# Even tokens first: loading queries and keys two tokens to a partition in a block-sparse attention and mixer kernel

## The chip, the cores and the metric

The kernel runs on one core of one Trainium2 chip. The metric is the device time of one execution in microseconds (us), as the median of several runs.

## The reference, cut to what matters

The inputs are `q`, `k` and `v` of 4 batches, 8 heads, 768 tokens and 64 numbers a head, and four mixer weights, all in float32. Attention is sparse by blocks of 64 tokens. Each query scores the mean key of each of the 12 blocks, keeps the best three that are not in its future, and always keeps its own block. Inside the kept blocks it attends causally.

```
k_rep = k.reshape(B, H, n_blocks, block, D).mean(axis=3)
gate_scores = np.einsum('bhsd,bhnd->bhsn', q, k_rep)        # future blocks: -1e9
top_idx = np.argsort(gate_scores, axis=-1)[..., -top_k:]    # and the own block
scores = scale * np.matmul(q, k.transpose(0, 1, 3, 2))      # masked by block and causally
x = softmax(scores) @ v                                     # then x: (batch, 768, 512)
u = x + (relu(x.transpose(0, 2, 1) @ w_tok1) @ w_tok2).transpose(0, 2, 1)
out = u + relu(u @ w_ch1) @ w_ch2
```

The order of the 768 tokens inside the chip's memories is free as long as queries, keys, values, masks, the token weights and the stores agree on it.

## The kernel before, in words

The work is cut into 16 pairs of heads (two heads of one batch, four pairs to a batch). A pair is first prepared and then attended.

Preparation (`prepare`, called for each pair): `load_qk` (L312) loads keys and then queries of both heads in float32 on SP's queue, 128 tokens to a tile and one token to a partition, so that each contiguous piece in memory is one token of one head, 256 bytes; it issues one transfer for each head. `transposes` (L358) turns six tiles on TensorE, `evac_t` (L367) copies them out on ScalarE, and `cast` (L376, GpSimd) or `cast_act` (L383, ScalarE, pair 0 alone) writes the two heads in half precision into the slots `KA` and `QA`. `ksum` (L388) sums keys by block on VectorE and `kcopy` (L396) places the sums of the two heads. The gate follows: `gate_q` (L406, pair 0), `gate` with `gate_s` and `gate_r` (L415 to L435, single pairs), or `gate_t`, `gate_e` and `gate_b` (L437 to L463) for a group of two or four pairs (`GROUPED`, L49). On VectorE `gm` (L465) adds the bias for future blocks, `top` (L482) takes the eight largest of 12 gate scores, ten times a pair, `below` (L492) compares with the third, and `bias` (L503) makes mask numbers. `mask` (L513) transposes them on TensorE, and `put_mask` (L522) writes them as 24 extra rows below the queries; `indicator` (L337) has put matching rows below the keys, so that one matmul gives scores with the block mask in them. The first 128 queries need no mask, so there are five gate tiles (`GJ`).

Attention (`attend`): for each head, `scores` (L529) in three groups of key tiles, `expo` (L547) on ScalarE, `diag` (L555) for the causal corner of the diagonal tiles on VectorE (for pair 0 TensorE adds the corner `tri`), `av` (L563) with the values and a column of ones, `recip` and `norm` (L575, L583). `load_v` (L322) loads the values on GpSimd's queue and casts them on the way.

The mixer runs by batch: `tok1`, `relu1`, `umix`, `uadd` over tokens (in columns for batch 0), a transpose of `u` (on TensorE for batch 0, by DMA with `turn_u` after that), and `ch1`, `relu2`, `ch2`, `oadd`, `store` over channels. Token weights come in two transfers on GpSimd's queue, the first and second that L732 and L733 issue.

The order of all instructions is written out when the program is built: `plan` (L113) is a list scheduler with a cost and a priority for each operation, its own model of the transfers (`transfers`, L84) and of the buffer rings. Each engine then runs its instructions in that order. The mixer of batch 0 fills TensorE under later pairs. `AHEAD` (L27) says how far the first four pairs are prepared ahead of their attention; `VAFTER` (L44) says after which cast the load of each pair's values may be issued, and `WAIT` (L50) does it for the weights. In the first microseconds `dummy` (L721) matmuls on a constant tile fill TensorE's holes.

```
T[t32, i] = t
for g in range(2):
    nc.sync.dma_start(out=t[:, :, D * g:D * g + D], in_=src[b, h + g].rearrange("(j p) d -> p j d", p=128))
```

Of the kernel before, what the change touches and what calls it, by code (L numbers as in the profile page):

```python
# [26 lines left out]
AHEAD = 2.5  # L27
LATER = 1.0
R = 5
# [10 lines left out]
def QACT(i):  # L40
# [3 lines left out]
VAFTER = [("kt", 1), ("kt", 2), ("qt", 2), ("qt", 3), ("qt", 3), ("qt", 4), ("qt", 6), ("qt", 8),  # L44
          ("qt", 11), ("qt", 12), ("qt", 13), ("qt", 14), ("kt", 15), ("qt", 15), ("qt", 15), ("qt", 15)]
DIRECT = (0,)
WSIZE = (2400, 4500)
GATE = {1: 400, 2: 1000, 3: 1000, 4: 1000}
# [174 lines left out]
def kernel(  # L223
# [23 lines left out]
    GJ = NJ - 1  # L247
# [25 lines left out]
    ks2 = [sp.tile([128, 32], FP, tag=f"ks{r}", name=f"ks{r}") for r in range(R)]  # L273
    bn16 = [sp.tile([128, GJ, 128], F16, tag=f"bn{y}", name=f"bn{y}") for y in range(NBN)]
    w1_16 = sp.tile([128, NJ, DT], F16, tag="w1", name="w1")
    w2_16 = sp.tile([128, 2, S], F16, tag="w2", name="w2")
    wc1_16 = sp.tile([128, NCC, DC], F16, tag="wc1", name="wc1")
    wc2_16 = sp.tile([128, NFC, DM], F16, tag="wc2", name="wc2")
    own4 = sp.tile([128, 4 * GJ, 2 * NB], FP, tag="own4", name="own4")
    gbias = sp.tile([128, GJ, 2 * NB], FP, tag="gbias", name="gbias")  # L280
    gown = sp.tile([128, 3 * GJ * NB], FP, tag="gown", name="gown")
    gone = gown[:, 0:GJ * NB].rearrange("p (j n) -> p j n", n=NB)
    own = gown[:, GJ * NB:].rearrange("p (j c) -> p j c", c=2 * NB)
# [5 lines left out]
    gt = sp.tile([128, S - 128], FP, tag="gt", name="gt")  # L289
# [22 lines left out]
    def load_qk(i, t32, src):  # L312
        b, h = pairs[i]

        def f():
            t = sb(t32, [128, NJ, 2 * D], FP, f"{t32}_{i}")
            T[t32, i] = t
            for g in range(2):
                nc.sync.dma_start(out=t[:, :, D * g:D * g + D], in_=src[b, h + g].rearrange("(j p) d -> p j d", p=128))
        return f  # L320

    def load_v(i):  # L322
        b, h = pairs[i]

        def f():
            nc.gpsimd.dma_start(out=V16[i % (R + 1)].rearrange("p g j d -> p (g j) d")[:, :, 0:D],  # L326
                                in_=v[b, h:h + 2].rearrange("g (j p) d -> p (g j) d", p=128))
        return f
# [5 lines left out]
    def twice(t):  # L334
        return t.rearrange("p j (x n) -> p j x n", x=1).broadcast_to([128, GJ, 2, NB])

    def indicator(r):  # L337
        if r:
# [3 lines left out]
        nc.vector.tensor_scalar(out=KAX[64:MK, r].rearrange("q x s -> q (x s)").bitcast(FP).rearrange("q (m w) -> q m w", w=32),  # L342
                                in0=ident32[64:MK, 64:MK].rearrange("q (m w) -> q m w", w=1).broadcast_to([2 * NB, 2 * NB, 32]),
                                scalar1=ONES, scalar2=None, op0=ALU.mult)

    def own_four():
        for c in range(4):
            nc.gpsimd.tensor_copy(out=own4[:, c:4 * GJ:4, :], in_=own)
        nc.gpsimd.tensor_copy(out=gbias.rearrange("p j (x n) -> p j x n", n=NB), in_=twice(gone))
# [8 lines left out]
    def transposes(t32, i):  # L358
        def f():
            p = ps("big", None, f"t{t32}")  # L360
            T["tr", t32, i] = p
            t = T[t32, i]
            for j in range(NJ):
                nc.tensor.transpose(out=p[:, 128 * j:128 * j + 128], in_=t[:, j, :], identity=ident32)  # L364
        return f
# [10 lines left out]
    def cast(dst, name, i, x):  # L376
        def f():
            lo = 64 * x
            to, src = dst[i % R][x][0:64, :], T[name, i][lo:lo + 64, :]
            nc.gpsimd.tensor_copy(out=to, in_=src)  # L380
        return f

    def cast_act(dst, name, i, x):  # L383
        def f():
# [635 lines left out]
```

## Time and profile before

| what | us |
|---|---|
| median of three runs (263.88 to 265.19) | 264.51 |
| the profiled execution | 264.1 |
| its span, first to last instruction | 262.4 |
| TensorE matmul busy | 253.8 |
| VectorE busy | 158.1 |
| ScalarE busy | 146.4 |
| GpSimd busy | 79.8 |

The span is the part of the execution that the profile divides up; 1.7 us of the profiled execution lie around it. Engines overlap, so busy times don't add up to the span. Names: PE is TensorE's matmul, PEld its weight load, DVE VectorE, ACT ScalarE, POOL GpSimd, SP the engine that issues the loads of queries and keys and the stores; a "q" after an engine marks its issuing of transfers. Matmuls are pipelined, so that a busy PE still may have room. L364 is line 364 of the kernel. A row of the timeline gives the start, the length, the engine, the line, the operation, the tiles written and read with their sizes, and the count of instructions that were merged.

### The profile page before, as it was taken

The page shows a single profiled execution, that of the slowest core. Times are in us where ns is not written, and L with a number is a line of the kernel's source. Part 1 is how long each engine was busy: PE and PEld are TensorE (multiplying, and loading weights), DVE is VectorE, ACT ScalarE, POOL GpSimd, SP SyncE. Part 2 cuts the span into 40 slices and gives each one's busy share as a digit, 9 for nine tenths or more (in the row PEclk, how much of TensorE's full clock was granted, in tenths as well). Part 3 has the DMA queues.
Part 4 walks back from the last instruction along what each step waited for, and adds up shares of the span by engine and source line. Part 5 has one row for each costly group of instructions (what it writes and reads, how often), then busy time and mean ns, then how long its engine had stood idle before and what let it go on. Part 6 is the DMA issues. An engine that isn't in the chain of part 4 may idle for free.

```text
span 262.4 us, 5901 instructions
## 1 busy us (share of the span) xinstructions
PE 253.8 (97%) x2330; PEld 162.8 (62%) x2330; DVE 158.1 (60%) x539; ACT 146.4 (56%) x200; POOL 79.8 (30%) x112
## 2 busy tenths in 40 slices
PE   7999899999999999899999999999999999999994
PEld 7977588885776685566655766544455544466443
DVE  4569869998966499886598566462243253333222
ACT  3886998877899669677617999410034400044000
POOL 8299628974557462640730000000000000000000
PEclk9999999999999999999999999999999999999999
DMA  8999999999999974493193000008220035300032
GB/s 166 224 171 204 203 185 192 184 197 190 204 183 170 209 151 30 32 142 91 10 169 106 2 2 0 2 0 200 80 82 0 0 65 138 130 30 2 0 146 95
DMA packets 91323, 28.78 MB, mean 110 GB/s; under 512 B 84896, under 2 KB 87840, under 8 KB 91296
## 3 DMA queue, kind: packets, MB, share of 16 engines
q1 hardware_dynamic: 63232, 21.33, 38.5%
q0 software_dynamic: 28064, 7.08, 27.6%
q8 instruction: 18, 0.29, 0.5%
q14 instruction: 9, 0.07, 0.1%
HBM read 26.83 MB, written 6.29 MB: 126 GB/s over the span
## 4 chain that ended last, share of the span: by engine, by line
PE 74%; DVE 15%; DMA 5%; ACT 2%; issue 2%; POOL 1%; DVEq 0%; ACTq 0%
PE c L704 21%; PE c L683 20%; PE sps L539 10%; PE avp L571 6%; DMA V<-in_v_dram 5%; DVE QA L525 3%; DVE m L489 3%; PE avp L721 3%; PE ups L614 3%; PE tql L364 2%; PE tok L602 2%; PE tkl L364 2%; ACT e L552 1%; PE gtp L443 1%; DVE e L559 1%
## 5 line engine op out<-in xcount | busy, mean ns | idle before, releaser
L552 ACT ACTIVATE e<-sps 128x1024 f16<-128x1024 f32 (+1 forms) x96 | 84.0, 919 | 19.0 <-PE sps L539 18.1
L683 PE MATMUL c<-uT,wc 128*128 128x256 f16 (+1 forms) x384 | 69.9, 326 | 0.9 <-DVE QA L525 0.7
L704 PE MATMUL c<-wc,h 128*128 128x512 f16 (+2 forms) x300 | 64.8, 370 | 0.0
L693 ACT ACTIVATE h<-c 128x512 f16<-128x512 f32 x48 | 28.7, 598 | 58.0 <-PE c L683 57.7
L683 PEld LDWEIGHTS <-wc 128*128 128x128 f16 x384 | 36.5, 97 | 24.6 <-issue 1.1
L539 PE MATMUL sps<-QA,KA 88*128 88x512 f16 (+3 forms) x256 | 50.8, 306 | 0.9 <-ACT e L552 0.8
L704 PEld LDWEIGHTS <-h 128*128 128x128 f16 x300 | 28.8, 98 | 31.3 <-issue 0.6
L380 POOL CAST KA<-kt 64x768 f16<-64x768 f32 x30 | 25.1, 837 | 41.4 <-ACT kt L373 30.8
L712 DVE TENSOR_TENSOR ob<-u,c 128x512 f32<-128x512 f16 (+2 forms) x25 | 16.6, 666 | 34.8 <-PE c L704 34.7
L695 DVE TENSOR_SCALAR h<-c 128x256 f16<-128x256 f32 x48 | 20.3, 424 | 27.8 <-PE c L683 27.7
L559 DVE TENSOR_TENSOR e<-e,m 128x256 f16<-128x256 f16 x90 | 29.2, 333 | 13.1 <-ACT e L552 12.5
L539 PEld LDWEIGHTS <-KA 88*128 88x128 f16 x256 | 22.6, 98 | 17.1 <-issue 1.5
L380 POOL CAST QA<-qt 64x768 f16<-64x768 f32 x30 | 25.3, 842 | 11.5 <-ACT qt L373 10.1
L571 PE MATMUL avp<-V,e 128*128 128x65 f16 x672 | 26.7, 193 | 1.3 <-DVE e L559 0.9
L571 PEld LDWEIGHTS <-e 128*128 128x128 f16 x672 | 25.4, 97 | 3.8 <-DVE e L559 1.1
L373 ACT COPY kt<-tkl 128x768 f32<-128x768 f32 x16 | 12.8, 798 | 10.5 <-PE tkl L364 6.8
L393 DVE TENSOR_REDUCE kst<-kt 128x12 f32<-128x768 f32 x16 | 15.0, 945 | 6.0 <-ACT kt L373 5.9
L590 DVE TENSOR_TENSOR x<-avp,rc 128x384 f16<-128x384 f32 x32 | 17.8, 555 | 0.6
L326 POOL DMA_DIRECT2D V<-in_v_dram x16 | 16.4, 1030 | 0.0
L525 DVE COPY QA<-bps 24x640 f16<-24x640 f16 x32 | 14.2, 480 | 1.1 <-PE bps L519 0.8
L373 ACT COPY qt<-tql 128x768 f32<-128x768 f32 x16 | 12.8, 801 | 2.6 <-PE tql L364 2.4
L622 DVE TENSOR_TENSOR u<-x,ups 128x512 f16<-128x512 f16 x18 | 11.6, 683 | 3.9 <-PE ups L614 3.8
(75 smaller groups left out, 212.9 us busy)
## 6 DMA issues: line engine op xcount, KB each, us to landing
kl<-in_k_dram SPq DMA_DIRECT2D x32, 192.0 KB, 5.3
ql<-in_q_dram SPq DMA_DIRECT2D x32, 192.0 KB, 5.4
out_dram<-ob SPq DMA_DIRECT2D x23, 256.0 KB, 2.0
V<-in_v_dram POOLq DMA_DIRECT2D x16, 192.0 KB, 6.3
wc<-in_moe_w_ch_dram POOLq DMA_DIRECT2D x8, 384.0 KB, 8.4
w<-in_moe_w_tok_dram POOLq DMA_DIRECT2D x2, 384.0 KB, 8.4
out_dram<-ob SPq DMA_DIRECT2D x1, 160.0 KB, 1.8
out_dram<-ob SPq DMA_DIRECT2D x1, 96.0 KB, 1.7
```

Of the source, the lines that this page charges most:

```text
L373: nc.scalar.copy(out=t, in_=p[:, 0:S])
L380: nc.gpsimd.tensor_copy(out=to, in_=src)
L525: nc.vector.tensor_copy(out=QA[i % R][x][64:MK, 128:S], in_=T["bps", gi][32 * s:32 * s + 2 * NB, :])
L539: nc.tensor.matmul(out=p[:, off + a:off + a + n], lhsT=KA[i % R][x][0:MK, 128 * kk:128 * kk + 128], rhs=QA[i % R][x][0:MK, q0 + a:q0 + a + ...
L552: nc.scalar.activation(out=e[:, 0:width], in_=T["sps", i, x, g][:, 0:width], func=AF.Exp, scale=scale)
L559: nc.vector.tensor_tensor(out=d, in0=d, in1=m0.rearrange("p (a b) -> p a b", a=1).broadcast_to([128, 2, 128]), op=ALU.mult)
L571: nc.tensor.matmul(out=p[:, jq, :], lhsT=T["e", i, x, g][:, o:o + 128], rhs=V16[i % (R + 1)][:, x, kk, :], start=(kk == 0), stop=(kk == jq))
L590: nc.vector.tensor_tensor(out=T["x16", b][:, :, 64 * hh:64 * hh + 64], in0=T["aps", i, x][:, :, 0:64], in1=T["rc", i, x].broadcast_to([128 ...
L683: nc.tensor.matmul(out=p, lhsT=wc1_16[:, cc, 128 * fc:128 * fc + 128], rhs=T["uT", b][:, cc, a // 128:e // 128, :], start=(cc == 0), stop= ...
L693: nc.scalar.activation(out=T["h2", b][:, fc, a:e], in_=T["c1", b, fc, n], func=AF.Relu)
L695: nc.vector.tensor_scalar(out=T["h2", b][:, fc, a:e], in0=T["c1", b, fc, n], scalar1=0.0, scalar2=None, op0=ALU.max)
L704: nc.tensor.matmul(out=T["c2", b, j, lo], lhsT=T["h2", b][:, fc, 128 * j:128 * j + 128], rhs=wc2_16[:, fc, lo:hi], start=(fc == 0), stop=( ...
```

## The change

A 128-token tile now holds the even tokens of its 128 in its first 64 places and the odd ones in the last 64. Queries and keys of a pair come in one transfer for each tensor. A partition receives two neighbouring tokens of one head as one piece of 512 bytes, and a row of a loaded tile has even-token numbers in columns 0 to 63 and odd-token numbers in columns 64 to 127. A transposed tile therefore has even tokens on partitions 0 to 63 and odd ones on 64 to 127, for one head, where it had the two heads before. A cast now takes one parity of both heads, and writes 64-column runs.

All that meets tokens follows: values, the rows of `w_tok1` and the stores are cut in two by parity, one transfer each; `w_tok2` is loaded as it is and reordered on GpSimd (`turn_w2`). Key sums are made per 32 pairs of tokens, exchanged between partition halves and added (two more small reduces in `kcopy`). A gate tile now holds 128 token pairs of one head, with 12 columns for the even and 12 for the odd token, so there are six instead of five (`NM`), with twelve runs of `top` for ten; `gm` and `bias` work pair by pair inside a group, and the copies `own4` and `gbias` (`own_four` on GpSimd) are gone. `tri` and `m0` are each made in two halves. In the planner, costs follow, `AHEAD` goes from 2.5 to 3.0, five entries of `VAFTER` name earlier casts, and casts wait for the scores of both heads of the old pair.

The diff, cut to its core:

```diff
-AHEAD = 2.5
+AHEAD = 3.0
-VAFTER = [("kt", 1), ("kt", 2), ("qt", 2), ("qt", 3), ("qt", 3), ("qt", 4), ("qt", 6), ("qt", 8),
-          ("qt", 11), ("qt", 12), ("qt", 13), ("qt", 14), ("kt", 15), ("qt", 15), ("qt", 15), ("qt", 15)]
+VAFTER = [("kt", 1), ("kt", 2), ("qt", 2), ("qt", 3), ("qt", 3), ("kt", 4), ("qt", 5), ("qt", 6),
+          ("qt", 10), ("qt", 11), ("qt", 13), ("qt", 14), ("kt", 15), ("qt", 15), ("qt", 15), ("qt", 15)]
...
-            t = sb(t32, [128, NJ, 2 * D], FP, f"{t32}_{i}")
+            t = sb(t32, [128, NM, 2 * D], FP, f"{t32}_{i}")
             T[t32, i] = t
-            for g in range(2):
-                nc.sync.dma_start(out=t[:, :, D * g:D * g + D], in_=src[b, h + g].rearrange("(j p) d -> p j d", p=128))
+            nc.sync.dma_start(out=t, in_=src[b, h:h + 2].rearrange("g (c p t) d -> p (g c) (t d)", p=128, t=2))
...
-            nc.gpsimd.dma_start(out=V16[i % (R + 1)].rearrange("p g j d -> p (g j) d")[:, :, 0:D],
-                                in_=v[b, h:h + 2].rearrange("g (j p) d -> p (g j) d", p=128))
+            for t in range(2):
+                nc.gpsimd.dma_start(out=V16[i % (R + 1)][64 * t:64 * t + 64].rearrange("p g j d -> p (g j) d")[:, :, 0:D],
+                                    in_=v[b, h:h + 2].rearrange("g (j p t) d -> t p (g j) d", p=64, t=2)[t])
...
-            to, src = dst[i % R][x][0:64, :], T[name, i][lo:lo + 64, :]
-            nc.gpsimd.tensor_copy(out=to, in_=src)
+    def half(dst, i, t):
+        return dst[0:64, i % R].rearrange("p x (j t w) -> p (x j) t w", t=2, w=64)[:, :, t, :]
+    def cast(dst, name, i, t):
+        return lambda: nc.gpsimd.tensor_copy(out=half(dst, i, t), in_=pairs_of(name, i, t))
...
+            for lo in (0, 64):
+                nc.vector.tensor_reduce(out=kst[lo:lo + 64, :, 1], in_=kst[64 - lo:128 - lo, :, 0:1], axis=AX.X, op=ALU.add)
             for lo, c in ((0, 0), (64, NB)):
...
+            for s, i in enumerate(GROUPED[gi]):
+                nc.vector.tensor_tensor(out=a[:, s].rearrange("p (t m n) -> p t m n", t=2, n=NB),
+                                        in0=T["gps", i].rearrange("p m (t n) -> p t m n", n=NB),
+                                        in1=gown[:, 0].rearrange("p (t m n) -> p t m n", t=2, n=NB), op=ALU.add)
...
-            for j in range(GJ):
-                for x in range(2):
-                    nc.vector.max(out=t[:, j, s, x, :], in_=T["gm", gi][:, j, s, NB * x:NB * x + NB])
+            for r in range(2 * NM):
+                nc.vector.max(out=T["m8", gi][:, s, r, :], in_=T["gm", gi][:, s, NB * r:NB * r + NB])
...
-            for j in range(GJ):
-                nc.tensor.transpose(out=p[0:n, 128 * j:128 * j + 128], in_=bn16[gi % NBN][:, j, 0:n], identity=ident16)
+            for m in range(NM):
+                t, c = m // (NM // 2), m % (NM // 2)
+                nc.tensor.transpose(out=p[0:n, 256 * c:256 * c + 256].rearrange("q (h t w) -> q t h w", h=2, t=2)[:, t], in_=bn16[gi % NBN][:, m, 0:n], identity=ident16)
...
-        return lambda: nc.sync.dma_start(out=out[b, 128 * j:128 * j + 128, lo:hi], in_=T["ob", b, j, lo][:, 0:hi - lo])
+            for t in range(2):
+                nc.sync.dma_start(out=out[b, 128 * j:128 * j + 128, lo:hi].rearrange("(p t) c -> t p c", t=2)[t],
+                                  in_=T["ob", b, j, lo][64 * t:64 * t + 64, 0:hi - lo])
...
+    def load_w1():
+        for t in range(2):
+            nc.gpsimd.dma_start(out=w1_16[64 * t:64 * t + 64], in_=w1[t])
+    def turn_w2():
+        nc.gpsimd.tensor_copy(out=w2_16.rearrange("p g (j t w) -> p (g j) t w", t=2, w=64),
+                              in_=w2_in.rearrange("p g (j w t) -> p (g j) t w", t=2, w=64))
...
-                O["cast", name, i, x] = op("POOL", occ, occ + 55, [O[name, i]] + last_scores(x), pre + 4 + off,
+                O["cast", name, i, x] = op("POOL", occ, occ + 55, [O[name, i]] + last_scores, pre + 4 + off,
...
-    own_op = op("POOL", 1240, 1280, [], 30.0, own_four)
+    w2_op = op("POOL", 1700, 1760, [W[1]], 5.0, turn_w2)
```

## The prediction

> **What bounds the kernel now.** I read the shares of the page first, then busy time by stretch of the run, then the first 14 us of the timeline, then the chain that ended last, then the end of the timeline.
>
> ```profile
> PE 253.8 (97%) x2330; PEld 162.8 (62%) x2330; DVE 158.1 (60%) x539; ACT 146.4 (56%) x200; POOL 79.8 (30%) x112
> ```
>
> PE looks full, but part of that is the warming matmul of L721. The stretches (us; PE, PEld, DVE, ACT, POOL busy with instruction counts, clock, DMA share, GB/s), then the same view for L721 alone (PE, PEld):
>
> ```profile
> 20.00:30.00 10.00, 9.02 (x135) 6.53 (x133) 9.18 (x43) 7.68 (x10) 9.73 (x13) 1.00 1.62 204
> 36.00:60.00 24.00, 24.00 (x351) 20.01 (x350) 22.25 (x76) 19.98 (x29) 19.13 (x27) 1.00 1.28 192
> 60.00:90.00 30.00, 29.46 (x296) 19.82 (x295) 21.45 (x78) 25.58 (x35) 16.74 (x20) 1.00 1.21 191
> 90.00:110.00 20.00, 18.77 (x160) 12.89 (x159) 18.30 (x76) 14.57 (x21) 9.32 (x11) 1.00 0.66 84
> 175.00:262.00 87.00, 83.97 (x446) 43.23 (x444) 27.70 (x52) 15.52 (x26) 0.00 (x0) 1.00 0.24 73
> ```
> ```profile
> 0.00:5.00 5.00, 3.64 (x34) 3.38 (x34) 1.00 0.71 148
> 5.00:14.00 9.00, 3.98 (x60) 3.58 (x61) 1.00 1.30 223
> 14.00:36.00 22.00, 2.67 (x32) 1.91 (x29) 1.00 1.48 188
> ```
>
> So PE has spare time only before 36 us and a little at 90-110. From 175 us it is solid channel mixing, which the edit hardly touches. Any time gained or lost must appear as PE idle time before 175 us, as more PE work, or after the last matmul. DVE is the second full engine: 92% and 93% at 20-30 and 36-60. The start:
>
> ```profile
> 4.99 0.84 PE L364 MATMUL tkl<-id,kl 128*128 128x128 f32 x6
> 8.51 1.25 PE L411 MATMUL gps<-ks,qt 128*128 128x24 f32 x10
> 12.22 0.88 DVE L525 COPY QA<-bps 24x640 f16<-24x640 f16 x2 [0.57 <-PE bps L519]
> 14.06 1.03 ACT L552 ACTIVATE e<-sps 128x1024 f16<-128x1024 f32 x1
> ```
>
> Keys of pair 0 arrive at 5 us; gate, mask and evacuations put the first exponential at 14.06. Later the chain that ended last (start, us, what) has one load in it:
>
> ```profile
> 72.65 12.38 DMA V<-in_v_dram
> ```
>
> **What the Trainium skill says.** "DMA: Bandwidth & Descriptors", Specifications, puts line rate at pieces of 512 B or more. The trace agrees in direction: in the window 2-14 us, where nearly all pieces are of 256 B, the queues moved 229 GB/s; in the window 250-262 us, where 2 KB rows are stored, the best slice reaches 403 GB/s.
>
> ```profile
> DMA packets 10639, 2.74 MB, mean 229 GB/s; under 512 B 10510, under 2 KB 10638, under 8 KB 10638
> ...
> GB/s 150 369 362 21 0 0 0 0 0 0 0 0 0 0 7 362 403 144 355 403 75 0 0 0 0 0 0 0 27 225 348 294 7 162 350 298 64 0 0 0
> ```
>
>  The same page, Rules for kernel authors, says that two transfers to disjoint partition halves serialize, so the split values, `w_tok1` and stores buy no bandwidth and cost issue time; no run here shows that yet. "SBUF — State Buffer", Who interferes with whom, says VectorE with two SBUF inputs blocks against GpSimd reads. The trace agrees: L497 took 0.28 us alone and 0.82 at 18.66, beside a GpSimd cast.
>
> **Part by part.**
>
> *Loads of q and k.* 393 KB (two 192 KB transfers) at 229 GB/s takes 1.72 us. At 229 GB/s a 256-byte piece costs one of 16 engines 17.9 ns; a 2 KB piece at 403 GB/s costs 81 ns. A straight line gives 26.9 ns for 512 B, hence 305 GB/s and 1.29 us. Bounds: 1.72 (no gain) and 0.98 (store rate). SP issues one transfer instead of two; two cost 1.04 us for `kl` of pair 0. So the first keys come 0.4 + 0.5 = 0.9 us sooner, the first queries 1.3.
>
> *Start of pair 0.* Two more L401 reduces of slightly larger shape (155 ns, taken as 190): +0.4 us. Two more of the ten gate matmuls (1.25 us): +0.2. Two more of ten MAX8 (0.82 us): +0.16. Mask tile of six transposes for five (0.45): +0.05. Three tensor operations of 144 columns for 120, at 283 ns: +0.08. The gate waited for queries (7.53 + 0.80 = 8.33) and not for key sums (7.69 + 0.33 = 8.02), so 0.3 of the 0.4 hides. Mask: -0.9 + 0.1 + 0.5 = -0.3. But ACT had one evacuation (13.36-14.16) in front of the first exponential; its keys now land over 2 us sooner, so that goes. First exponential about 1.0 us sooner.
>
> *VectorE per pair.* +0.4 key sums, +0.16 maxima, +0.08 rest: 0.64 us, about 10 us over 16 pairs. In 36-60 the view of that line shows four key sums and two runs of maxima: +2.1 us against 1.75 us idle there. Against that, the first mixing weights (issued at 24.8 after the casts of pair 3, used at 34.8) come some 3 us sooner, so one token-mixing column (12 matmuls 0.67, 12 more 0.67) and its two VectorE additions (0.55 each) move into the holes of 26-36. Net on the start of channel mixing (59 us): -1.0 + 0.4 = -0.6 us. Bounds -2 and +2.
>
> *Values.* L326 becomes two issues; 1.03 us becomes 1.3 (bounds 1.1 and 2.06), on GpSimd, behind which casts and weights queue. GpSimd is 80% busy at 36-60 and nobody waits long; 0. If that cover goes, scores of the next pair wait: 0.3 us a pair. The value load of pair 7 is freed from the casts of pair 8 (`VAFTER`), so the 12.38 us row should go. PE waited only 0.39 + 0.16 us: -0.5. Bounds 0 and -2 (attention, stopped 2.8 us, keeps more mixing in hand).
>
> *GpSimd otherwise.* `own_four` (1.3 us) goes; `turn_w2` comes, twice a cast's elements (1536 for 768 at 0.84): 1.7 us, bounds 1.6 and 3. It stands between the second weight (landed 34.7) and its use at 39.0: 4.3 us of slack, 0. Four selects instead of two at the start (0.29 and 0.60): under 1 us, ahead of indicators that no one needs before pair 1; 0. Casts, two halves of strided columns: 0 (bounds -0 and +0.1 each). A key cast now waits for both heads of the old pair; 0.
>
> *TensorE.* Nine masks with one more transpose at 55 ns (five end to end in 0.28 before the tail): 0.5. Three groups with one more transpose at 0.11: 0.3. Gate columns narrow from 64 to 32 in five gates: -0.1. Sum +0.7, and PE is full there.
>
> *Groups.* A group of four now does four additions and four mask operations instead of one each: 4 x 0.31 - 0.66 = +0.6, 4 x 0.31 - 0.80 = +0.4, maxima +0.66, key sums +1.6: +3.2 us of VectorE in two bursts (90-106 and 130-141), +1 in the pair of 6 and 7. The first burst already cost PE 1.23 us of its 20. I take +0.4 for each; bounds 0 (mixing fills it) and 3.
>
> *Stores.* Each is two issues, 0.42 us apart (259.21 to 259.63). No matmul waits for them until the end:
>
> ```profile
> 257.99 2.02 SPq L716 DMA_DIRECT2D out_dram<-ob  x3
> 258.69 0.75 DVE L712 TENSOR_TENSOR ob<-u,c 128x320 f32<-128x320 f16 x2 [0.73 <-PE c L704]
> ```
>
> The last 320 columns' second issue pushes the last 192 columns by 0.4, and their own second issue adds 0.4: +0.8, all after the last matmul. Bounds 0.4 and 1.2.
>
> **Sum.** -0.6 - 0.5 + 0.7 + 0.8 + 0.8 = +1.2 us. The profiled execution took 264.1 us, of which 262.4 are its span; 265.3 on that scale. The median of the runs, 264.51, lies 0.4 above it. I forecast 265.5, as the two scales differ by less than the spread of the three runs.
>
> **Rivals.**
>
> *B, VectorE decides (slower).* Place: from the first mask to the start of channel mixing, and the two bursts. If the holes at 10-20 and 30-38 lie where pairs wait for ACT, eight preparations cost 8 x 0.64 = 5.1 us, of which two hide: -1.0 + 3.1 = +2.1; bursts 2 x 0.9; PE 0.7; end 0.8; values -0.5: +4.9, or some +3.5 when mixing absorbs half of the bursts: 268. It decides once VectorE's extra before 59 us exceeds its idle time there (4.3 us after 20 us). For it: 92-93% busy. Against: loads come early enough to start preparations in VectorE's idle stretches, and mixing can fill PE after 60 us.
>
> *C, the loads carry through (faster).* Head -1.3, weights fill the holes of 26-36 for -1.5, pair 7 and the hole behind it -1.4, PE and end +1.5: -2.7, so 261.8. For it: PE spends 2.7 us in L721 after 14 us, and the DMA engines are oversubscribed (share above 1). Against: keys of pair 4 landed by 21 us and were transposed at 35.5, so beyond pair 3 loads were not what was late.
>
> *D, the pieces are no faster.* If 512 B went at 229 GB/s the issue alone would gain 0.5 and the costs stay: +2.5; part of B's chance.
>
> **Chances.** Forecast 0.42 (own range 264.3 to 266.7), B with D 0.34, C 0.24. A measurement of this kernel tells 0.5%, 1.3 us, from no change: faster is below 263.2, slower above 265.8. C gives 0.22 faster and 0.02 same; the forecast 0.27 same and 0.15 slower; B 0.30 slower and 0.04 same. Faster 0.22, same 0.33, slower 0.45. The range 261.6 to 268.8 takes in both rivals' times; beyond it lie the outer bounds of bursts and head.
>
> **What would show it.** Right: `kl` transposes near 4.1 us, first exponential near 13, a hardware queue with half of the 63232 packets, VectorE near 168 us busy, no load row in the chain, the last store landing 0.8 us later after the last matmul. Wrong: channel mixing starting well before 57 or after 62 us; PE idle over 3 us at 90-110; strided casts over 0.95 us.

## The result and the profile after

| | before | after |
|---|---|---|
| median, us | 264.19 (263.61 to 265.19) | 273.04 (272.41 to 274.67) |
| profiled execution, us | 264.1 | 274.67 |
| its span, us | 262.4 | 273.0 |

The ratio is 1.034, with a 95% interval of 1.0283 to 1.0398: slower by 8.9 us where the forecast had +1.2 on the profiled execution (a median of 265.5), and outside the range of 261.6 to 268.8. The profiled execution of the changed kernel is the longest of its four, so the medians carry the sums below and the profile shows places.

Shares of the page, then the hardware and the software queue (packets, MB, share of 16 engines), of the changed kernel:

```profile
PE 257.5 (94%) x2308; PEld 164.5 (60%) x2308; DVE 170.7 (63%) x617; ACT 146.4 (54%) x200; POOL 89.1 (33%) x127
...
q1 hardware_dynamic: 38544, 21.39, 35.3%
q0 software_dynamic: 28336, 7.08, 35.3%
```

VectorE works 12.6 us more. The hardware queue has fewer packets (38544 for 63232), since the pieces of queries and keys are twice as long. The software queue, which carries values and weights, moved the same 7.08 MB, but its packets took 35.3% of the engines' time, against 27.6% of a shorter span before. The bytes are the same; what the diff changes on that queue is that values and `w_tok1` go out in halves of 64 partitions, each half reading every second token.

The stretches of the changed kernel (us; PE, PEld, DVE, ACT, POOL; clock, DMA share, GB/s):

```profile
20.00:30.00 10.00, 8.03 (x78) 5.48 (x77) 6.64 (x45) 4.99 (x7) 9.75 (x14) 0.68 2.52 161
36.00:60.00 24.00, 22.83 (x335) 19.12 (x335) 20.85 (x74) 19.75 (x29) 17.31 (x22) 1.00 1.10 178
60.00:90.00 30.00, 27.11 (x270) 19.12 (x269) 27.56 (x100) 22.29 (x30) 18.59 (x24) 1.00 1.12 199
90.00:110.00 20.00, 20.00 (x205) 14.75 (x204) 15.95 (x85) 14.27 (x21) 7.14 (x9) 1.00 0.30 51
175.00:262.00 87.00, 86.98 (x508) 45.21 (x507) 31.94 (x66) 21.58 (x35) 0.00 (x0) 1.00 0.30 61
```

Between 20 and 30 us everything but GpSimd is slack: 78 matmuls for 135 before, VectorE 6.6 us for 9.2, the clock at 0.68. The DMA engines are busier than before (2.52 for 1.62) and move less (161 GB/s for 204). At 60 to 90 us VectorE is 92% busy and PE loses 2.9 us where it lost 0.5. The start, by the timeline of the changed kernel:

```profile
4.38 1.51 PE L356 MATMUL tkl<-id,kl 128*128 128x128 f32 x6
8.73 1.49 PE L405 MATMUL gps<-ks,qt 128*128 128x24 f32 x12
13.93 0.88 DVE L507 COPY QA<-bps 24x640 f16<-24x640 f16 x2 [0.20 <-PE bps L501]
15.60 1.03 ACT L534 ACTIVATE e<-sps 128x1024 f16<-128x1024 f32 x1
...
24.43 1.34 PE L553 MATMUL avp<-V,e 128*128 128x65 f16 x21 [1.97 <-DMA V<-in_v_dram]
```

Keys are there 0.6 us sooner, but in this execution their six transposes take 1.51 us for 0.84, and the first exponential is 1.5 us later. Then PE stands 1.97 us for the first values. The chain that ended last has that load in it, and the waits of PE from 14 to 130 us (total, times, longest) put VectorE next:

```profile
15.31 9.08 DMA V<-in_v_dram
```
```profile
PE avp L553 <- DMA V<-in_v_dram: 2.0, 1, 2.0
PE ups L596 <- DVE u L604: 1.5, 1, 1.5
PE sps L521 <- DVE gm L465: 1.2, 1, 1.2
PE avp L553 <- DVE e L541: 1.0, 1, 1.0
```

The end of the run, timeline of the changed kernel:

```profile
266.86 3.66 SPq L700 DMA_DIRECT2D out_dram<-ob  x6
267.57 0.75 DVE L694 TENSOR_TENSOR ob<-u,c 128x320 f32<-128x320 f16 x2 [0.73 <-PE c L686]
```

The last three stores hold SP for 3.66 us, where three issues in 2.02 us were enough before. After the last matmul 5.1 us of the span are left (267.9 to 273.0), for 3.4 before (259.0 to 262.4).

### The profile page after: what moved, and what is told of

The parts are those of the page before. It is cut to its first block, busy times and chain, and to the rows that moved or that the text cites. A ratio compares the mean times of both kernels' runs of the same rounds, so it can differ in the third digit from the quotient of the medians.

```text
span 273.0 us, 5955 instructions
## 1 busy us (share of the span) xinstructions
PE 257.5 (94%) x2308; PEld 164.5 (60%) x2308; DVE 170.7 (63%) x617; ACT 146.4 (54%) x200; POOL 89.1 (33%) x127
## 3 DMA queue, kind: packets, MB, share of 16 engines
q1 hardware_dynamic: 38544, 21.39, 35.3%
q0 software_dynamic: 28336, 7.08, 35.3%
## 4 chain that ended last, share of the span: by engine, by line
PE 72%; DVE 18%; DMA 3%; ACT 2%; issue 1%; POOL 1%; DVEq 0%; ACTq 0%
PE c L686 23%; PE c L665 19%; PE sps L521 10%; PE avp L553 7%; DVE kst L384 3%; DMA V<-in_v_dram 3%; PE ups L596 3%; DVE QA L507 2%; PE avp L707 2%; DVE m L475 2%; PE tok L584 2%; PE tkl L356 2%; DVE e L541 2%; DVE ks L393 1%; DVE x L572 1%; DVE kst L391 1%
## 5 line engine op out<-in xcount | busy, mean ns | idle before, releaser
L534 ACT ACTIVATE e<-sps 128x1024 f16<-128x1024 f32 (+1 forms) x96 | 83.9, 918 | 20.4 <-PE sps L521 15.5
L665 PE MATMUL c<-uT,wc 128*128 128x256 f16 (+1 forms) x384 | 69.2, 325 | 0.4 <-ACT h L675 0.2
L665 PEld LDWEIGHTS <-wc 128*128 128x128 f16 x384 | 36.7, 97 | 23.6 <-issue 0.8
L686 PEld LDWEIGHTS <-h 128*128 128x128 f16 x300 | 28.5, 98 | 30.4 <-issue 0.6
L375 POOL CAST KA<-kt 64x768 f16<-64x768 f32 x30 | 24.9, 829 | 47.4 <-PE sps L521 27.6
L541 DVE TENSOR_TENSOR e<-e,m 128x256 f16<-128x256 f16 x90 | 30.2, 350 | 15.1 <-ACT e L534 14.6
L553 PE MATMUL avp<-V,e 128*128 128x65 f16 x672 | 28.1, 197 | 3.2 <-DMA V<-in_v_dram 2.0
L553 PEld LDWEIGHTS <-e 128*128 128x128 f16 x672 | 26.6, 100 | 6.6 <-DMA V<-in_v_dram 2.2
L324 POOL DMA_DIRECT2D V<-in_v_dram x32 | 24.2, 766 | 0.2 <-issue 0.2
L384 DVE TENSOR_REDUCE kst<-kt 128x24 f32<-128x768 f32 x16 | 15.1, 948 | 4.0 <-ACT kt L365 3.8
L475 DVE MAX8 m<-gm 128x8 f32<-128x12 f32 x192 | 15.0, 153 | 0.2
```

What stands on the lines that cost most here:

```text
L324: nc.gpsimd.dma_start(out=V16[i % (R + 1)][64 * t:64 * t + 64].rearrange("p g j d -> p (g j) d")[:, :, 0:D], in_=v[b, h:h + 2].rearrange(" ...
L375: return lambda: nc.gpsimd.tensor_copy(out=half(dst, i, t), in_=pairs_of(name, i, t))
L384: nc.vector.tensor_reduce(out=kst[:, :, 0], in_=T["kt", i].rearrange("p (n w) -> p n w", w=32), axis=AX.X, op=ALU.add)
L475: nc.vector.max(out=T["m8", gi][:, s, r, :], in_=T["gm", gi][:, s, NB * r:NB * r + NB])
L534: nc.scalar.activation(out=e[:, 0:width], in_=T["sps", i, x, g][:, 0:width], func=AF.Exp, scale=scale)
L541: nc.vector.tensor_tensor(out=d, in0=d, in1=m0.rearrange("p (a b) -> p a b", a=1).broadcast_to([128, 2, 128]), op=ALU.mult)
```

## The experiments

The theory that I took into the first eight runs was rival B's. VectorE's added work sets the time, the second store issues add their part at the end, and the new order of the loads makes the first values late. Its rivals were the new order alone, and the loads. Each kernel below has one base, and its time is compared with 264.2 us of the kernel before or 273.0 of the changed one.

### VectorE's work

`after_dve_lean` takes the exchange copies and half of the maxima out of the changed kernel; a block's key sum then holds half of its tokens, and one third-best score serves two tokens.

```diff
-            for lo in (0, 64):
-                nc.vector.tensor_reduce(out=kst[lo:lo + 64, :, 1], in_=kst[64 - lo:128 - lo, :, 0:1], axis=AX.X, op=ALU.add)
...
-            for r in range(2 * NM):
+            for r in range(NM):
                 nc.vector.max(out=T["m8", gi][:, s, r, :], in_=T["gm", gi][:, s, NB * r:NB * r + NB])
...
```

> The changed kernel with its order unchanged, but with the two exchange reduces of each pair left out and six runs of MAX8 in place of twelve, each third value serving two gate rows (so the gate is not the reference's). VectorE loses about 0.4 + 0.9 us a pair, some 14 us, a little more than the change added. Theory V, that VectorE's added work is on the chain that sets the end: 5 to 7 us less than the changed kernel's 273, most of it between 40 and 120 us. Theory L, that the late first values and the cold clock at 20 to 30 us cost most: 0 to 2 us less.

Measured: 269.92 us, ratio 1.0201 (1.014 to 1.0261), 3.1 us less than the changed kernel, between the two theories. VectorE is busy for 157.9 us, 12.9 less, about as much as the change had added. PE still waits 2.4 us for the first values.

`before_dve_extra` puts scratch work of that kind (VectorE 165.5 us busy, 7.4 more) into the kernel before, with the order of everything else as it was.

```diff
+            for lo in (0, 64):
+                nc.vector.tensor_reduce(out=xtra[64 - lo:128 - lo, 0:NB], in_=kst[lo:lo + 64, :].rearrange("p (n o) -> p n o", o=1), axis=AX.X, op=ALU.add)
...
+            for x in range(2):
+                nc.vector.max(out=xtra[:, 32 + 8 * x:40 + 8 * x], in_=T["gm", gi][:, 0, s, NB * x:NB * x + NB])
```

> The kernel before with its order unchanged and idle VectorE work added where the change adds it: two more small reduces with the key sums and two more MAX8 with each run of ten, into a scratch tile: 2 x 0.16 + 2 x 0.08 = 0.48 us a pair, 7.7 us in all. Theory V: 3 to 5 us more than 264.2. Theory L: 0 to 1.5 us more.

Measured: 268.66 us, ratio 1.0166 (1.013 to 1.0201): +4.5 us for 7.4 us of work, as theory V had it. The rows that the added work imitates are these, of the changed kernel (count, busy us, mean ns):

```profile
L475 DVE MAX8 m<-gm 128x8 f32<-128x12 f32 x192 | 15.0, 153 | 0.2
L393 DVE TENSOR_REDUCE ks<-kst 64x24 f32<-64x48 f32 x32 | 6.3, 197 | 1.0
L391 DVE TENSOR_REDUCE kst<-kst 64x24 f32<-64x24 f32 x32 | 5.5, 173 | 1.0
```

So VectorE's work costs by itself. In the kernel before, 0.6 of the added time reaches the end; taken out of the changed kernel alone, 0.24 of it comes back (3.1 of 12.9 us).

### The stores

`after_store_whole` stores each tile in one issue, with the rows of the output in the permuted order. So it undoes two things at once: the halves, and the writing of every second row.

```diff
-            for t in range(2):
-                nc.sync.dma_start(out=out[b, 128 * j:128 * j + 128, lo:hi].rearrange("(p t) c -> t p c", t=2)[t],
-                                  in_=T["ob", b, j, lo][64 * t:64 * t + 64, 0:hi - lo])
+            nc.sync.dma_start(out=out[b, 128 * j:128 * j + 128, lo:hi], in_=T["ob", b, j, lo][:, 0:hi - lo])
```

> The changed kernel with each store as one transfer of 128 partitions (rows then come out in the order of the tile, even tokens first). The gap from the last matmul to the end is 3.7 us before and 5.1 after. Theory S, that this gap is the second issues alone: 1.4 us less than 273, all of it after the last matmul. If the stores' row pitch caused it, nothing changes but the issue count, and the gain is under 0.5 us.

Measured: 271.89 us, ratio 1.0284 (1.0226 to 1.0343), 1.2 us less, near theory S; with four executions each the two spreads still overlap (270.43 to 273.14, and 272.41 to 274.67). The span ends 3.4 us after the last matmul again. The same stretch of the end (258 to 273 us) by the view of the transfers, first for the stores in halves, then whole:

```profile
DMA packets 1120, 1.57 MB, mean 105 GB/s; under 512 B 224, under 2 KB 480, under 8 KB 1120
...
q1 hardware_dynamic: 1120, 1.57, 46.9%
...
out_dram<-ob SPq DMA_DIRECT2D x9, 128.0 KB, 2.4
```
```profile
q1 hardware_dynamic: 1008, 1.57, 28.5%
...
out_dram<-ob SPq DMA_DIRECT2D x4, 256.0 KB, 2.0
```

Equal bytes, nothing else on the queues, and 1.6 times the engines' time (46.9% for 28.5%). Over all stores of the run a row of 2 KB took 146 ns on the mean in the halves and 91 whole. A half lands in 2.4 us, a whole one in 2.0. It is not the writing of every second row: `before_all_costs` below stores halves of 64 rows that follow each other, and its last 15 us (the same 1120 packets) show 44.8%. I took note of the 1.2 us alone then; it was a sign of the main cause.

### The loads of queries and keys, and the settings of the order

`before_load512` and `before_load512_two` give the kernel before the 512-byte pieces, in one transfer or in one for each head; the tokens of queries and keys are then mixed up. The diff is that of the first; the second keeps the loop over `g`, with `t[:, 3 * g:3 * g + 3]` as the target.

```diff
-            for g in range(2):
-                nc.sync.dma_start(out=t[:, :, D * g:D * g + D], in_=src[b, h + g].rearrange("(j p) d -> p j d", p=128))
+            nc.sync.dma_start(out=t, in_=src[b, h:h + 2].rearrange("g (c p t) d -> p (g c) (t d)", p=128, t=2))
```

> The kernel before, its order unchanged, with queries and keys loaded as the change loads them: one transfer of 384 KB, 512-byte pieces, two tokens of a head to a partition (the rest takes the tile as it was, so the attention is of mixed tokens). Only the loads change. Theory L, that larger, earlier loads push the values back: 1 to 3 us more than 264.2, with a hole before the first value matmul. Theory V: the loads alone help or do nothing: 0 to 1.5 us less.

> The kernel before with 512-byte pieces but still one transfer for each head (two issues on SyncE's queue for a pair's keys or queries; token order in the values left as before, so tokens are mixed up). With both in one transfer it took 0.6 us less than the kernel before. If the size of the pieces did that: 263.4 again. If the number of issues did: 264.1. The first keys land at 4.5 us in the first case; at 4.8 in the second.

Measured: 263.47 us, ratio 0.9966 (0.9948 to 0.9984), and 263.38 us, ratio 0.9968 (0.995 to 0.9985). The pieces bring 0.7 to 0.8 us; one issue less brings nothing that shows. That the larger loads push the values back (theory L) is out.

`after_load256` is the changed kernel with the old two transfers of 256-byte pieces (the diff above turned round; tokens mixed up again).

> The changed kernel, its order unchanged, with queries and keys loaded as before: two transfers of 192 KB with 256-byte pieces (again of mixed tokens). Theory L: 1 to 3 us less than 273. Theory V: 0 to 1.5 us more, since the loads are then late for the changed order.

Measured: 276.9 us in the profiled execution, 3.9 more than the changed kernel's median and more than either theory had; 283.9 to 286.3 in three others, which are not compared. The profile has PE waiting 4.0 us after 14 us for keys and queries. As far as one execution tells, the changed order needs the faster pieces.

`before_new_settings` has `AHEAD` and `VAFTER` of the change on the kernel before, `after_old_settings` the old ones on the changed kernel, `before_load512_settings` the new ones with 512-byte pieces.

```diff
-AHEAD = 2.5
+AHEAD = 3.0
...
-          ("qt", 11), ("qt", 12), ("qt", 13), ("qt", 14), ("kt", 15), ("qt", 15), ("qt", 15), ("qt", 15)]
+          ("qt", 10), ("qt", 11), ("qt", 13), ("qt", 14), ("kt", 15), ("qt", 15), ("qt", 15), ("qt", 15)]
```

> The kernel before with the planner's settings of the change alone: AHEAD 3.0 and its VAFTER. If the settings suit only the changed loads, 1 to 4 us more than 264.2 (another order of the head). Theories V and L both say within 1 us.

> The changed kernel with AHEAD 2.5 and the VAFTER of before. If the settings carry a part of the loss, 1 to 3 us less than 273; if they were made for the changed costs, 0 to 3 us more. Theories V and L both say within 1 us.

> The kernel before with only the 512-byte loads and the new order settings (AHEAD 3.0, the new list of value loads); key sums and order of tokens left as before, so the tokens that are attended to are mixed up, and the instructions are the same. Theory (the +9.5 us of the new settings on the kernel before came from its slower loads, which they ask for too soon): 263 to 266, no holes of 5 us for keys and 2 us for queries between 58 and 67 us. Rival (the settings themselves are bad for an instruction stream of the old costs): 268 to 274.

Measured: 273.58 us, ratio 1.0332 (1.0283 to 1.038); 271.82, ratio 1.0295 (1.0241 to 1.0348); 263.45, ratio 0.9969 (0.9957 to 0.9982). With the old pieces the new settings cost 9.4 us, which no theory had, in one wait of 5.1 us for keys and one of 2.2 for queries. With the new pieces they cost nothing. On the changed kernel the old settings give 1.2 us back, with spreads that overlap (271.22 to 274.25). So the settings are not the cause; at most a small part is theirs.

`after_v0_early` lets the first value load go out ahead of the second pair's keys.

```diff
-VAFTER = [("kt", 1), ("kt", 2)
+VAFTER = [("kt", 0), ("kt", 2)
```

> The changed kernel with the values of pair 0 allowed after the casts of its own keys instead of those of pair 1, so some 4 us sooner in GpSimd's queue. Theory L: the hole of 2.1 us before the first value matmul and the slow clock after it go, 2.5 to 4 us less than 273. Theory V: the head shifts by up to 2 us, but VectorE's chain from 60 us takes back at least half: 0 to 1.5 us less.

Measured: 272.19 us, ratio 1.0301 (1.0234 to 1.0367), 0.9 less, which the spread covers (271.05 to 273.99). The wait for values goes, and waits of 1.6 us for keys, 1.8 for queries and 1.3 for the token weights come in its place: it only changes which load is late.

### The partition halves of the value loads

`before_v_split` splits the value loads of the kernel before, tokens in their order.

```diff
-            nc.gpsimd.dma_start(out=V16[i % (R + 1)].rearrange("p g j d -> p (g j) d")[:, :, 0:D],
-                                in_=v[b, h:h + 2].rearrange("g (j p) d -> p (g j) d", p=128))
+            for t in range(2):
+                nc.gpsimd.dma_start(out=V16[i % (R + 1)][64 * t:64 * t + 64].rearrange("p g j d -> p (g j) d")[:, :, 0:D],
+                                    in_=v[b, h:h + 2].rearrange("g (j p) d -> p (g j) d", p=128)[64 * t:64 * t + 64])
```

> The kernel before with each value load split into two halves of 64 partitions, as in the changed kernel, and nothing else (the order of the tokens stays). Theory (GpSimd has room; the split costs two issues of some 0.77 us instead of one of 1.0 us and no time at the end): 264 to 265. Rival (the values' second issue waits for slots of the queue and the first values come 2 us late): 266 to 267, with a PE wait for V near 21 us.

Measured: 272.82 us, ratio 1.0324 (1.0285 to 1.0363): +8.6 us, and both expectations fell. Here my theory fell too: the part that I had put at nothing costs about as much as the whole change. PE's waits of this kernel (15 to 110 us), and its stretch from 60 to 70 us:

```profile
PE tkl L365 <- DMA kl<-in_k_dram: 4.4, 1, 4.4
PE tql L365 <- DMA ql<-in_q_dram: 1.7, 2, 1.2
```
```profile
60.00:70.00 10.00, 5.84 (x43) 4.26 (x43) 3.55 (x9) 2.61 (x3) 3.12 (x4) 0.66 1.24 186
```

Not the values are late but the keys. PE does 43 matmuls there for 105 before, and its clock falls to 0.66. The damage was done up to 40 us earlier. By the packet records the two queues together had moved 0.03 MB less than in the kernel before by 20 us, 0.67 less by 30, and still 0.68 less by 60.

`before_v_by_head` makes as many issues of half the bytes, each over all 128 partitions.

```diff
+            for g in range(2):
+                nc.gpsimd.dma_start(out=V16[i % (R + 1)][:, g, :, 0:D], in_=v[b, h + g].rearrange("(j p) d -> p j d", p=128))
```

> The kernel before with each value load split into two issues by head: 32 issues of half the bytes as in the changed kernel, but each over all 128 partitions. Split by partitions it took 8.6 us more. If the number of issues (0.77 us each on GpSimd, with their place in the queue) made that: 270 to 273, with the wait for keys of over 4 us near 60 us. If the 64 partitions of each did (packets twice as long): 264 to 265.5.

Measured: 263.58 us, ratio 0.9978 (0.9959 to 0.9996). So the number of issues is innocent, though each by head holds GpSimd for 0.83 us and each half for 0.76; it is the 64 partitions. The transfers between 20 and 30 us of the kernel before, of `before_v_split`, of `before_v_by_head` and of the changed kernel (packets, MB, share of 16 engines; shares add to over 100% because each engine has several packets open at a time):

```profile
q0 software_dynamic: 3789, 0.75, 87.2%
q1 hardware_dynamic: 5048, 1.26, 73.1%
```
```profile
q0 software_dynamic: 3100, 0.39, 139.4%
q1 hardware_dynamic: 3902, 0.98, 92.0%
```
```profile
q1 hardware_dynamic: 6407, 1.61, 94.6%
q0 software_dynamic: 3336, 0.42, 65.9%
```
```profile
q0 software_dynamic: 4302, 0.75, 202.7%
q1 hardware_dynamic: 1673, 0.84, 48.2%
```

Read each as time per packet: 16 engines x 10 us x share / packets. By head a software packet takes 32 ns (65.9% of 160 us / 3336). By halves of the partitions it takes 72 ns. The packets of keys and queries beside them go from 24 ns to 38. Hence 1.37 MB moved in these 10 us against 2.03. In the changed kernel a software packet takes 75 ns (0.75 MB, weights among them), against 37 before for the same 0.75 MB.

The loss is one of this stretch and not of every half. By the trace's packet records, the 128-byte packets of the values alone took 73 ns on the mean in `before_v_split` from 20 to 30 us, for 32 by head; between 30 and 60 us they took 31 in both. What else must be under way for a half to be slow, the runs don't show.

`before_load512_v_split` joins the halves with the 512-byte loads (tokens of queries and keys mixed up).

> The kernel before with the 512-byte loads and the value loads split into halves of 64 partitions, and nothing else (tokens of queries and keys are mixed up against the values and the mask). With the 512-byte loads alone 263.4. If the split's cost is only that it starves the slow loads of queries and keys: 263.5 to 265 here. If it costs by itself: 267 to 272.

Measured: 265.87 us, ratio 1.0054 (1.0025 to 1.0084). That is 2.4 us over the 512-byte loads alone, above the first expectation's band and below the second's. The faster pieces leave room, so keys are no longer late; but the first values are, as in the changed kernel:

```profile
24.14 0.84 PE L571 MATMUL avp<-V,e 128*128 128x65 f16 x21 [2.82 <-DMA V<-in_v_dram]
```

`after_v_whole` takes the split out of the changed kernel (values' tokens in natural order).

```diff
-            for t in range(2):
-                nc.gpsimd.dma_start(out=V16[i % (R + 1)][64 * t:64 * t + 64].rearrange("p g j d -> p (g j) d")[:, :, 0:D],
-                                    in_=v[b, h:h + 2].rearrange("g (j p t) d -> t p (g j) d", p=64, t=2)[t])
+            nc.gpsimd.dma_start(out=V16[i % (R + 1)].rearrange("p g j d -> p (g j) d")[:, :, 0:D],
+                                in_=v[b, h:h + 2].rearrange("g (j p) d -> p (g j) d", p=128))
```

> The changed kernel with each value load in one transfer over 128 partitions again, as in the kernel before (the values' tokens then lie in their natural order, so they meet the wrong weights; the instructions are the same but for 16 fewer issues). Theory 1 (the split is the main cost: its packets took twice as long between 20 and 30 us, and the first values came 2 us late): 267 to 269 from 273.0, and no PE wait for V near 24 us. Theory 2 (with the faster loads there is room for it, and VectorE's work sets the time): 272 to 273.

Measured: 271.23 us, ratio 1.0255 (1.0216 to 1.0294). The wait for values is gone and the clock stays at 1.00, but only 1.8 us are won, between the two theories. Of PE's waits from 10 to 130 us, 5.9 us are now for VectorE and 1.3 for ScalarE, none for a load. From 20 to 30 us the software queue shows this:

```profile
q0 software_dynamic: 4111, 1.08, 135.6%
```

That is 53 ns a packet for 75 with the halves. It is not the 37 of the kernel before: more of its packets are weights of 512 bytes and over (941 for 675), and these take longer (99 ns for 61).

### The parts together

`after_three` joins `after_dve_lean`, `after_v0_early` and `after_store_whole`; `after_lean_v_whole` joins `after_dve_lean` and `after_v_whole`; `after_four` adds the whole stores to that.

> The changed kernel with three parts undone at once: VectorE without the exchange copies of the key sums and with six maxima rows per pair instead of twelve, value load 0 taken in ahead of the second pair's keys, and each store in one issue again (so key sums, maxima and the rows' order in the output are left incomplete or changed). Theory (VectorE's added work, the second store issues and the late first values are separate costs): the single runs gave -3.1, -1.1 and -0.9 us, so about 268 from 273.0. Rival 1 (they are one cost seen three times, since the later ones lie beside the first): about 270, as with the VectorE part alone. Rival 2 (the whole loss lies in these three): 264 to 265.

> The changed kernel with VectorE lean (no exchange copies, six maxima rows per pair instead of twelve) and the values in one transfer each; the stores stay split. Left out: part of the key sums and maxima; the values' tokens are in natural order. Theory (VectorE's work and the values' split hide each other, since both make the same stretch up to 120 us late; the stores are apart, at the end): 264.4 to 265. Rival (no interaction between these two; it is the stores that gain from the others): 267.5 to 268.5.

> The changed kernel with the value loads and the stores in one transfer each again and VectorE without the exchange copies and with six maxima rows per pair in place of twelve (values, order of the output and masks are then mixed up). What is left of the change: 512-byte loads, strided casts, the rows of the weights, the new order. With VectorE lean, early values and whole stores it was 266.5. Theory 1 (the split of the values is a large part of the loss): 263 to 265. Theory 2 (it isn't): 267 to 269, as the early values are not in it.

Measured: 266.8 us, ratio 1.0086 (1.0059 to 1.0114); 265.09 us, ratio 1.0035 (1.0021 to 1.005); 263.45 us, ratio 0.9964 (0.9949 to 0.998). The first fell between its theory and the rival that put the whole loss there; the other two came out as their first theories had it (the second 0.1 us above its band). With VectorE's work and both splits undone, nothing is left of the loss, and 0.7 us are gained, as by the 512-byte pieces alone. `w_tok1` is still loaded in halves in that kernel, so its split costs nothing that shows; the new order is still in it too.

`before_all_costs` goes the other way: the kernel before, in its own order, with 512-byte loads, the scratch work of `before_dve_extra`, the values split as in `before_v_split`, and the stores split like this (tokens of queries and keys mixed up).

```diff
-        return lambda: nc.sync.dma_start(out=out[b, 128 * j:128 * j + 128, lo:hi], in_=T["ob", b, j, lo][:, 0:hi - lo])
+        def f():
+            for t in range(2):
+                nc.sync.dma_start(out=out[b, 128 * j + 64 * t:128 * j + 64 * t + 64, lo:hi], in_=T["ob", b, j, lo][64 * t:64 * t + 64, 0:hi - lo])
+        return f
```

> The kernel before, in its own order, with 512-byte loads of queries and keys, values and stores each split into two halves of 64 partitions, and 7.7 us of scratch work on VectorE at the places of the exchange copies and maxima (tokens of queries and keys then mixed up). Theory (these four are the change; the new order neither saves nor costs): 271 to 274, by the sum -0.8, +2.4, +4.5, +1.1 = 271.4 and something for their interaction. Rival (the changed kernel's own order has a share of several us): 267 to 270.

Measured: 272.07 us, ratio 1.0286 (1.0254 to 1.0317). The loads and the three costs together make all but 1.0 us of the change.

Milestones from the timelines, us from the span's start, one profiled execution of each kernel:

| kernel | first exponential | first values used | first channel mixing | last exponential | last matmul |
|---|---|---|---|---|---|
| before | 14.1 | 21.6 | 59.3 | 164.1 | 259.0 |
| changed | 15.6 | 24.4 | 64.6 | 181.2 | 267.9 |
| VectorE lean | 15.3 | 24.1 | 64.8 | 177.1 | 263.7 |
| values whole | 15.3 | 22.5 | 61.0 | 177.6 | 264.3 |
| both | 15.5 | 21.8 | 59.0 | 171.4 | 258.1 |
| both, stores whole | 15.8 | 22.1 | 59.2 | 171.7 | 258.3 |
| before, with all costs | 14.0 | 24.0 | 64.3 | 171.2 | 266.1 |

The table shows why single undoings add to 6.1 us (3.1 + 1.8 + 1.2) and all of them to 9.6. At the start of channel mixing the late values hide VectorE's work: lean alone gains nothing there, but with the values whole it gains 2.0 (61.0 to 59.0). Taken out one after the other, the parts are 3.1 us for VectorE, then 4.8 for the values (269.92 to 265.09), then 1.6 for the stores (to 263.45), and what is left is 0.7 below the kernel before. In the other order VectorE is 6.1 (271.23 to 265.09) and the values 1.8. Each pair of numbers is the honest bracket; the runs give no single one. The lean kernel's four executions spread from 267.72 to 270.94, so its two steps are uncertain by one to two microseconds; the 1.6 of the stores, from 16 and 20 executions, is the surest.

## Why the prediction was wrong, step by step

**Loads: right.** 26.9 ns a piece and 305 GB/s were estimated; in `before_load512` a piece of 512 bytes took 27 ns by the median and 30 by the mean, and the changed kernel moved 295 GB/s from 2 to 14 us. Rival D is out. Rival C's direction was right for this part alone: 0.7 us.

**"First exponential about 1.0 us sooner": wrong, and harmless.** It came 1.5 later. Keys landed 0.6 us sooner, not 0.9. The transposes lost 0.7, but that varies between executions and is no part of the change. The clock's record starts, at full speed, at 6.57 us in this one, after the transposes, and at 4.96 in the kernel before. In `before_v_by_head`, with the old loads, it starts at 7.12 and they take 1.51 us too. In `after_v_whole` it starts at 4.21, they take 0.85 us, and the first exponential still comes at 15.3. What the sum left out is the interference that the prediction itself names. A GpSimd cast of the next pair now runs beside VectorE's mask numbers, which took 0.85 us for 0.28 (in `after_v_whole` two operations there took 0.96 and 0.75):

```profile
11.89 1.69 POOL L375 CAST KA<-kt 64x768 f16<-64x768 f32 x2 [4.00 <-ACT kt L365]
12.02 0.85 DVE L489 SCALAR_TENSOR_TENSOR bn<-gm,gown 128x144 f16<-128x144 f32 x1
```

The mask's transposes then began at 13.38 us, behind a query's transposes, where they began at 11.73 before. Yet `after_four` has its first exponential at 15.8 us and is faster than the kernel before, so the late start cost nothing that shows.

**"Values. [...] 0" and "-0.5": the step that failed most.** The price of the second issue was near (twice 766 ns for 1.3 us). The wait of pair 7 went, as said. In its place came one of 2.0 us for the first values, whose halves were issued at 14.4 and 15.3 us and landed at 22.1 and 24.4. The Trainium skill ("DMA: Bandwidth & Descriptors", Rules for kernel authors) says that two transfers to disjoint partition halves serialize and that one of 128 partitions should be used. I read it as "no gain in bandwidth" and put the cost at the issues alone. The runs show a loss: in the busiest stretch 72 ns for 32 a packet, and 38 for 24 for the traffic beside it. I gave no bound for that, though the window from 20 to 30 us was the one with the highest DMA share before (1.62). Cost: 1.8 to 4.8 us in the changed kernel, 2.4 beside 512-byte loads, 8.6 beside the old ones.

**"Net on the start of channel mixing [...] -0.6": wrong.** It began 5.3 us later, and the work of VectorE alone moved it by 2.7 (62.0 in `before_dve_extra`). The size of the work was not far off, 12.6 us for some 10. What failed is the offset, mixing work that would start some 3 us sooner and fill the holes of 26 to 36 us. In the changed kernel that stretch stood behind the late values, and token mixing began at 38.1 us for 34.8. With the values on time (`after_v_whole`) it began at 34.5, and channel mixing still at 61.0, 1.7 us later than before. Rival B named this place and mechanism; its terms for VectorE (3.1 and 1.8) are near the 3.1 to 6.1 measured. Its whole sum of +4.9 still fell short of 8.9, as it had the same -0.5 for the values.

**Groups, +0.4 each: too small and elsewhere.** PE is full from 90 to 110 us in the changed kernel. Its long holes after 60 us end on VectorE's work: 1.2 us at 72.6, 1.0 at 86.1 and 1.5 at 113.0, and VectorE is busy for over 90% of each.

**TensorE +0.7, GpSimd otherwise 0: right.** Without the warming matmuls PE is busy for 247.7 us in `after_four`, which has TensorE's new instructions and no long wait, and for 246.8 in the kernel before: +0.9. `turn_w2` took 1.46 us, nobody waited for it, and casts into strided columns took 829 and 843 ns as before (837 and 842).

**Stores +0.8: the place right, the size half.** I counted a second issue of 0.4 us. An issue of 64 partitions held SP for 0.47 to 0.59 us where most whole ones took 0.33, so a store costs some 1.1 us for 0.33, and each half lands later than a whole store did (2.4 us for 2.0). The tail grew by 1.7 us; undone, the stores gave 1.2 to 1.6 back.

In sum the terms -0.5, 0.2 and 0.8 for values, VectorE (start and groups) and stores measured 4.8, 3.1 and 1.6 in one order of undoing, and 1.8, 6.1 and 1.6 in the other. What is open: why the changed order, and not the old one, lets values and VectorE hide each other (on the kernel before the parts add up: -0.7 + 2.4 + 4.5 + 1.6 = 7.8, with the stores' 1.6 taken from the changed kernel; measured 7.8), and what the last 1.0 us between `before_all_costs` and the changed kernel is. A version that keeps the 512-byte pieces with values and stores in whole transfers and the natural order of tokens was not tried.

## What to carry to other kernels

A layout that interleaves partitions can be paid for in every transfer that must then be cut into partition halves. Price such a transfer in time per packet, in the stretch where the queues are fullest, and look for its victims in the other queue's loads too, even tens of microseconds later. Don't put added work at nothing on an engine that is over 90% busy in a stretch: here VectorE's cost 0.24 to 0.6 of its length, depending on what else was late. Undo suspected costs together as well as singly, and add them to the old kernel too, since one can lie in the shadow of another.

## What the runs showed of the hardware that I had not expected

Transfers of 64 partitions took longer for the same bytes. Stores of 2 KB rows, with nothing else on the queues at the end, took 146 ns a row for 91. Loads of 128-byte packets took 73 ns for 32 between 20 and 30 us, but 31 for 31 between 30 and 60 (`before_v_split` and `before_v_by_head`). Why, no view of the trace shows. Splitting by head, with all 128 partitions in each issue, was free (263.58 us for 264.2).

Waits of PE of 2.0 us and more in the first 70 us went with a stretch at half the clock. In the changed kernel the wait of 22.5 to 24.4 us went with half the clock from 23.6 to 30.5 (mean of 20 to 30 us: 0.68). In `before_v_split` a wait of 4.4 us went with half the clock from 62.3 to 69.1 (0.66 from 60 to 70). In `before_load512_v_split` one of 2.8 us went with 25.6 to 29.0 (0.83 from 20 to 30). No threshold comes out of these traces: after a wait of 1.4 us `after_store_whole` had such a stretch (23.5 to 30.3), and after one of 1.8 us `after_v0_early` had none. Nor is the clock what made the changed kernel slow: of its four executions the one with a mean clock of 0.999 took 273.36 us.
